# The mixing product of three quarters of the spectrum in rounded passes instead of exact fp32, with the hand-written order of all engines replaced

## The chip, the cores and the metric

The kernel runs on one core of one Trainium2 chip. The metric is the device time of one execution in microseconds (us). Five engines work side by side in the core: PE (TensorE, matrix products, with PEld for the loading of its stationary operand), DVE (VectorE), ACT (ScalarE), POOL (GpSimd) and SP, which issues DMAs here. They are held together by semaphores.

## The reference

```python
# spectral mixing, x: (8, 1856, 256)
X = np.fft.rfft(x, axis=1)
Yr = Xr @ w_r - Xi @ w_i + b_r
Yi = Xr @ w_i + Xi @ w_r + b_i
Y = soft_shrink(Yr, 0.01) + 1j * soft_shrink(Yi, 0.01)
y = np.fft.irfft(Y, n=1856, axis=1)
# mixture of experts over the 14848 tokens of y
# w_group gives one of 4 groups, w_expert one of its 4 experts
g_idx = np.argmax(x @ w_group, axis=1)
e_idx = np.argmax(xg @ w_expert[g], axis=1)
out[tok] = g_w * e_w * (np.maximum(x[tok] @ w1[g, e], 0) @ w2[g, e])   # F = 1024
```

All of it is float32. The kernel forms the complex product `Xr, Xi` by `w_r, w_i` with three real products: one common product of the difference of two spectra with `wc`, and two products of their own, of which one starts from the common one.

## The kernel before

**Work and stages.** The 8 batches are worked in 4 pairs. The transform of length 1856 is done as 58 by 32, in steps, each named by one letter. For a pair: `c` (`a_mm`, L339) and `d` (`a_turn`, L343) are the first small transform on PE and its transposition by DVE. Then come 8 units, each of two spectral positions (the last of one, so 15 positions a pair). For a unit, `e` (`f_mm`, L618) makes the spectrum on PE in a PSUM tile `bank`; `f` (`f_high`, ACT, L635) copies it rounded to fp32r (a rounded form that PE takes in one pass) into `xh`; `h` (`f_low`, DVE, L640) makes the rest `xl` = spectrum minus `xh`; `i` (`d_copy`, ACT, L645) and `g` (`d_sub`, DVE, L650) make `xd`, the fp32 difference for the common product. For a position, `j` (`m_bias`, ACT, L655) puts the bias into a PSUM tile `pw`; `y` (`m_common`, L661) adds the common product `xd` by `wc` with 2 fp32 matmuls of 256 columns; `z` (`m_share`, DVE, L666) copies it to the other half of `pw`; `k` (`m_mm`, L676) adds the two own products with 12 fp32r matmuls (high by high, high by low, low by high, for two halves of the 256 channels and two products); `m` (ACT, L682) and `o` (DVE, L687) do the shrinkage. With 15 positions in each of 4 pairs there are 60 common products.

After that a pair is transformed back: `r` (`b_mm`, L701), `s` (`b_turn`, DVE, L709), `v`, `w`, `x`. `G`, `H`, `R` route the tokens and `S` scatters their numbers into a list for each expert: 128 scatters on POOL, each an indirect DMA of 128 small rows (L248). The first 64 are tied to PE's steps (a scatter waits for the second last step of PE that was written ahead of it, and no more than 3 are on their way), the other 64 are not tied to PE and no more than 5 are on their way. `W`, `V`, `F`, `T`, `X`, `Y`, `U`, `A`, `B`, `D`, `E`, `J`, `K` are weights and 8 early jobs of the experts, begun while the spectrum is still being mixed. The rest of the experts' work follows in loops.

**What sets the order.** Up to about 536 us of the profile, each engine's order is that of a string `ORDER`, one letter a step; the loop over it calls the next step of that letter, and every instruction of the step goes to the end of its engine's queue. Nothing is reordered later, so an instruction that waits holds up all that is behind it on its engine.

```python
for c in ORDER.replace("\n", ""):
    next(steps[c])
```

The common product, whole:

```python
y = psum["m", pr, k][:, 0:D]
for h in range(2):
    nc.tensor.matmul(y, lhsT=units["xd", pr, k // 2][:, h, k % 2, 0], rhs=wc[:, h], start=False, stop=False, ...)
```

`pw`, `xd`, `xh` and `xl` each have two buffers.

Of the kernel before, what the change touches and what calls it, by code (L numbers as in the profile page):

```python
# [9 lines left out]
F32 = mybir.dt.float32  # L10
F32R = mybir.dt.float32r
# [3 lines left out]
ALU = mybir.AluOpType  # L15
# [3 lines left out]
NB, S, D = 8, 1856, 256  # L19
NA, NR = 58, 32  # L20
K1, KP = 30, 32
NP = NB // 2
# [15 lines left out]


ORDER = """  # L40
cddcdcdjcdcldcddcddQdjdcddddeQQfecffhhigiQgcQQyQydQzhkizfkdmmddehgiojfgccoyjyhddzkfdizmhdikgmgeoofccjddyjyhzdkizgkfmmhod
ijefgojcyyhzfkidzkmdgheiojgmocyfjyfhzihkgzikegdmmdoojfeyhjzfhiykigmzokgmjoeyjyzkzflfhikhmgoijefgfhmyzihioggkjemyojyfzhfk
zhiigkgmfmohrojssjfyizyhrkgigmssrzssokemfjfohjihrsyysgigcdcdczddvwxdklvdzwxclxvdkmodwjxxywvzwcxxwwxwddmcGddvoHRRRcRjefly
wxRRdRRhzwkkxefdimhimvRgRgRoRfcojxRwjddxRRRyywzRvwxwRzxvkkRRRwmxxwhRRiRRRmioRgjgRfGoeRRjHhyfRyfzRhzkRkhigRigeSemSSRRmRoo
jffRjyhRSzyRRRRkiShzRSRRRRmSkRReiSfggSojRhiygzSSSmiSRRoRkjgRRyfhmfoSRrzfjhhkiiRsygSgzrmRsskmrSsojeoSsRjyfshfzySrizkkhssi
ggmomvexjovwSwSjwyfxxwySfxzvhvxkwwxzkxSwxhmicwddigGSvomgjoHRxRwlScxRwvwdSjvRxyxSwRRyxedRSzzwcwSffxRhhvRiikwSmdSdRggRxkmS
wRxoRoeffRRRcRRRGdjdhjRRyihgRzSRRRyikzmRRRRHSSllkmReogRoSRfchRjfRidjRhcRySzdiSSygzRRgkkcRdSRmdRomoejRcydSRjdSRyffSzhkRSm
lldizhRdkoRgieSgjyRRRRRmozfRjhRfihSkRieSmggfRSoyjSfRhRhryiRzSiggSSskrzskmojSSssSmroyRssjzyrWezssWkSffhSWmivhixwvSkwgSwgx
vxeomwxSjovwxyVjxfzyhSzwfwSxSkihwkmgVixgmSeffohWjhiSoWgjViGvgvwHyxxyRRzwRxRzRkvwvRRxmRoxRIwRjwexRVyWRwzRRxwxkmoZRfFkRFRh
wGRRRigigRmjWoRRfjHRyhzyRRkmzRRRRRefoRhjRfkhyeSiSmgRzoSRkijRgyRfRmSSRRzokjRhSSSVfiRRShRRmgWySzRoiSSgSSVRRRkjmyRRzRVSRRRR  # L50
koTmSoXRYrUsRRsrASsSSBUSlSsrssVSrASWWUsSsvBSAxlWwSSvxvwxSwwSxwUxvxSwTxwxDBSwVVGWVVSAXIYWHvBxWwWwxRlRRvUxURvwVRRZFAxBwvDw
RAxEwRDWwRFVVxUBFxRURARRDAwVBRJBERRWDWWRRRxDTREXYRRDDRJJRUVEAKRVKRKlRURABBWTURFARWJSUWGVVVRSBXSSAYUBATUHDKRSRRRSDTRBlRWW
RSASRRREBRRUUAJRRKSBXSYSRRDRARDURABRVSUBRDAESUFFJRRBUVDRRRWWDEDVDRXAAWlRJYSREBVWBVTSSUJUWSKKASAVBSSSDBUAUADVSXBDDEBVYUSU
AEASDDSSSBBWUUSSVJSWAWBTSDJXDEAYJBSUEUVJVLADBKEJUAABDUKBDABDDDRKKEEKJKDMJEJKKK
"""

_OFF = {}
# [68 lines left out]
def spectral_moe(ctx: ExitStack, tc: tile.TileContext, x, wri, bri, wgate, w1, w2, cst, out):  # L126
    nc = tc.nc
# [23 lines left out]
    for n in (16,):  # L151
        t = keep.tile([128, NE, n], BF16, name=f"smask{n}")
# [143 lines left out]
    rt = inv.enter_context(tc.tile_pool(name="rt", bufs=1))  # L296
# [4 lines left out]
    cf = fwd.enter_context(tc.tile_pool(name="cf", bufs=1))  # L301
# [4 lines left out]
    T = cf.tile([128, K1, 64], F32, name="T")  # L306
    wf = fwd.enter_context(tc.tile_pool(name="wf", bufs=2))
    pw = fwd.enter_context(tc.tile_pool(name="pw", bufs=2, space=PSUM))

    def banks():  # L310
        return pa.tile([128, 2, 512], F32, name="bank")
# [41 lines left out]
    for _ in range(2):  # L353
        y = pw.tile([128, 512], F32, name="pw")
# [7 lines left out]
    wc = cf.tile([128, 2, D], F32, name="wc")  # L362
# [9 lines left out]
    def weight_steps():  # L372
        nc.scalar.copy(out=sl, in_=craw)
        yield
        nc.vector.tensor_tensor(out=wsum, in0=wraw, in1=wc, op=ALU.add)
        yield
        nc.vector.tensor_tensor(out=wraw, in0=wraw, in1=wc, op=ALU.subtract)
        yield
        for i, w_ in enumerate((wraw, wsum)):
            nc.scalar.copy(out=wh[:, i], in_=w_)  # L380
            yield
            nc.vector.tensor_tensor(out=wl[:, i], in0=w_, in1=wh[:, i].bitcast(F32), op=ALU.subtract)
            yield
        nc.vector.tensor_tensor(out=bias[:, D:], in0=bias[:, D:], in1=bias[:, 0:D], op=ALU.subtract)
        yield
# [10 lines left out]
    wg = ci.tile([128, 8, 64], F32, name="wg")  # L396
    nc.sync.dma_start(out=wg.rearrange("p c m -> p (c m)"), in_=wgate)
    late.close()
    zero = cf.tile([128, 128, 2], F32, name="zero")
    nc.gpsimd.memset(zero, 0.0)  # L400
    with tc.issue_after(x1.ins):
        nc.sync.dma_start(out=lst[0:NE * CAP].rearrange("(p j c) k -> p j (c k)", p=128, j=16),
                          in_=zero[:, 0:CAP // 128].rearrange("p c k -> p (c k)").unsqueeze(1).broadcast_to([128, 16, CAP // 64]))
# [151 lines left out]
    wts, raws, low, units, vs, psum = {}, {}, {}, {}, {}, {}  # L555
# [5 lines left out]
    def steps_of(*dims):  # L561

        def wrap(fn):
            def run():
                for idx in np.ndindex(*[len(d) for d in dims]):
                    fn(*[d[i] for d, i in zip(dims, idx)])
                    yield
            return run()
        return wrap
# [9 lines left out]
    pairs, later, u16, u8, two, k15 = range(NP), range(1, NP), range(16), range(8), range(2), range(15)  # L579

    def load_steps():
        for pr in later[1:]:
            for dc in range(4):
                x_in[pr, dc] = t = xp.tile([128, 32, 64], F32, name="xt")
                nc.sync.dma_start(out=t, in_=x_v[pr, dc])
                yield
        for e in range(NF + 1):
            for i, src in enumerate((w1, w2)):
                raws[e, i] = t = xp.tile([128, 2048], F32, name="xt")
                ins = nc.sync.dma_start(out=t, in_=src[e * 128:e * 128 + 128])  # L590
# [31 lines left out]
    def side(ins, what, pr, kk, h):  # L622
        apart(ins, (what, pr, kk, h), *((o_, pr, kk, 1 - h) for o_ in ("hs" if what in "fc" else "fc")))

    def quad(pr, kk, h):
        return quads(psum["f", pr, kk], kk)[:, h]
# [21 lines left out]
    def d_sub(pr, kk, h):  # L648
        t = units["xd", pr, kk][:, h, 0:min(2, 15 - 2 * kk), 0]
        side(nc.vector.tensor_tensor(out=t, in0=quad(pr, kk, h)[:, :, 0], in1=t, op=ALU.subtract), "s", pr, kk, h)  # L650

    @steps_of(pairs, k15)
    def m_bias(pr, k):
        psum["m", pr, k] = y = pw.tile([128, 512], F32, name="pw")
        nc.scalar.copy(out=y[:, 0:D], in_=bias[:, 0:D])  # L655

    @steps_of(pairs, k15)
    def m_common(pr, k):
        y = psum["m", pr, k][:, 0:D]
        for h in range(2):  # L660
            nc.tensor.matmul(y, lhsT=units["xd", pr, k // 2][:, h, k % 2, 0], rhs=wc[:, h], start=False, stop=False, skip_group_check=True)  # L661

# [230 lines left out]
        store(units.pop(("y", n, t)), lev[j, e], t, "out")  # L893

    w = STAT // 128
    first = []
    xp2 = ctx.enter_context(tc.tile_pool(name="xp2", bufs=3, side="right"))

    @steps_of(range(1))
    def last_lists(_):  # L900
# [7 lines left out]
    def first_rows(_):  # L908
# [2 lines left out]
        nc.gpsimd.tensor_copy(out=first[0].gi, in_=first[0].ent[:, :, 0])  # L911

    steps = dict(
        Q=weight_steps(), l=load_steps(), c=a_mm, d=a_turn, e=f_mm, f=f_high, h=f_low, i=d_copy, g=d_sub, j=m_bias, y=m_common, z=m_share, k=m_mm,
        m=m_relu, o=m_shrink, r=b_mm, s=b_turn,
        v=p_mm, w=p_out, x=p_turn,
        G=g_mm, H=g_turn, R=route_steps(), S=scatter_steps(), W=w_high, V=w_low, I=list_load, Z=list_convert, F=e_fetch, T=e_turn, X=e_high,
# [2 lines left out]
    by_hand = ExitStack()  # L920
    by_hand.enter_context(tc.manual_schedule(engines=engines))
    with ExitStack() as ph, tc.manual_schedule(engines={mybir.EngineType.Pool}):
        done = 0
        for c in ORDER.replace("\n", ""):
            next(steps[c])
            done += c == "o"
            if c == "o" and done == NP * 15:
                fwd.close()
                early["hp"] = ph.enter_context(tc.tile_pool(name="hp", bufs=2))
                early["mp"] = ph.enter_context(tc.tile_pool(name="mp", bufs=1))  # L930
                yp.append(ph.enter_context(tc.tile_pool(name="yp", bufs=6)))
                early["pp"] = ph.enter_context(tc.tile_pool(name="pp", bufs=2, space=PSUM))
        assert not pend and all(next(g, None) is None for c, g in steps.items() if c != "S")
        wts = {e: views(w) for e, w in wts.items()}
# [281 lines left out]
    for i, (kind, q) in enumerate(jobs):  # L1216
# [5 lines left out]
        if i + 2 < len(jobs) and jobs[i + 2][0] == "h":  # L1222
            k = jobs[i + 2][1] + KF - KH
            jw[i + 2], jids[i + 2] = half_load(slice(k, k + 1))
        if i + 1 < len(jobs) and jobs[i + 1][0] == "r":
            k, part = jobs[i + 1][1]
# [49 lines left out]
    with tc.For_i(KF, nfx, 1) as iv:  # L1276
# [9 lines left out]
        hts, h = [], hq.tile([128, 8, 256], F32, name="hh")  # L1286
# [43 lines left out]
```

## Time and profile before

| | before |
|---|---|
| median of 3 runs | 1176.19 us (1174.16 to 1179.11) |
| profiled execution, its own time | 1176.28 us |
| its span in the trace | 1174.5 us |
| mean granted clock of PE | 0.963 |
| PE busy | 1080.0 us, 92% of the span |
| DVE, ACT, POOL busy | 668.8, 482.0, 400.2 us |

The profiled execution stands 0.09 us above the median, and its span leaves 1.8 us of its time outside. PE is the engine to look at: where it stands idle or works slowly, the end may move. A busy share is an average over stages, so the stages are read apart below.

### The profile page before, as it was taken

What the parts mean: (1) busy time and instruction counts of PE and PEld (TensorE: products, weight loads), DVE (VectorE), ACT (ScalarE), POOL (GpSimd) and SP (SyncE); (2) the same over time, 40 slices, a digit from 0 to 9 for tenths busy, and PEclk for the clock granted to TensorE, in tenths of its full rate; (3) what the DMA queues carried; (4) which work ended last, traced back from release to release, by engine and by line L of the source; (5) the groups of instructions that cost most, each with busy time, mean ns of one, the idle gap of its engine ahead of it and who ended that gap; (6) DMA issues with size and microseconds to landing.
All of it is one profiled execution on the core that took longest, in us unless ns stands there. A gap on an engine that the chain in (4) does not pass through costs nothing. (4 is left out here: it accounts for less than half of the span.)

```text
span 1174.5 us, 23221 instructions
## 1 busy us (share of the span) xinstructions
PE 1080.0 (92%) x8944; PEld 896.6 (76%) x8944; DVE 668.8 (57%) x1572; ACT 482.0 (41%) x1222; POOL 400.2 (34%) x497
## 2 busy tenths in 40 slices
PE   7999979988966599879999999999999999999996
PEld 4786755755754378768989999887888888888995
DVE  6779846866765375435655454544554345544532
ACT  2453523532632253223455354444544345443532
POOL 0000132343343526545325333443425333343311
PEclk9999979998998699989999999999999999999999
DMA  9504301620230252104315131553324433313100
GB/s 386 156 3 177 113 1 38 174 72 10 96 105 1 84 205 63 61 28 137 120 56 178 43 112 46 193 193 103 121 85 139 185 113 116 110 52 110 48 23 25
DMA packets 39793, 119.83 MB, mean 102 GB/s; under 512 B 16998, under 2 KB 19305, under 8 KB 31618
## 3 DMA queue, kind: packets, MB, share of 16 engines
q1 hardware_dynamic: 19042, 70.32, 17.4%
q0 software_dynamic: 15744, 31.08, 8.6%
q10 hardware_dynamic: 4896, 16.93, 3.7%
q8 instruction: 71, 1.16, 0.4%
q14 instruction: 40, 0.33, 0.1%
HBM read 84.23 MB, written 34.61 MB: 101 GB/s over the span
## 5 line engine op out<-in xcount | busy, mean ns | idle before, releaser
L540 PE MATMUL py<-big,hh 128*128 128x512 f32 (+1 forms) x848 | 301.0, 396 | 0.0
L478 PE MATMUL ph<-xth,big 128*128 128x384 f32 (+3 forms) x992 | 272.2, 350 | 2.8 <-DVE hl L484 1.2
L541 PE MATMUL py<-big,hl 128*128 128x256 f32 (+1 forms) x848 | 237.1, 280 | 0.0
L248 POOL DMA_INDIRECT lst<-ent,sloti x128 | 126.9, 991 | 294.9 <-PE pw L676 166.0
L484 DVE SCALAR_TENSOR_TENSOR hl<-ph,hh 128x256 fp32r<-128x256 f32 x496 | 159.8, 366 | 81.9 <-ACT hh L482 72.1
L478 PEld LDWEIGHTS ph<-xth,big 128*128 128x128 f32 x992 | 181.1, 188 | 17.1 <-PE ph L478 2.5
L540 PEld LDWEIGHTS py<-big,hh 128*128 128x128 f32 (+1 forms) x848 | 155.8, 184 | 38.1 <-issue 1.6
L482 ACT ACTIVATE hh<-ph 128x256 fp32r<-128x256 f32 x496 | 143.7, 351 | 95.3 <-PE ph L478 88.3
L478 PE MATMUL ph<-xtl,big 128*128 128x384 f32 (+3 forms) x496 | 173.2, 349 | 0.3 <-DVE xtl L466 0.3
L541 PEld LDWEIGHTS py<-big,hl 128*128 128x128 f32 (+1 forms) x848 | 156.1, 184 | 0.2
L525 POOL DMA_INDIRECT out_dram<-yo,si_r x92 | 93.2, 1013 | 174.8 <-DVE yo L548 147.6
L548 DVE SCALAR_TENSOR_TENSOR yo<-py,ent_r,yo 128x256 f32<-128x256 f32 (+1 forms) x92 | 44.4, 483 | 180.6 <-ACT yo L547 166.6
L443 POOL DMA_INDIRECT xg<-ys_d,gi_r x92 | 89.7, 975 | 163.0 <-PE pg L461 129.4
L547 ACT ACTIVATE yo<-py,ent_r 128x256 f32<-128x256 f32 (+1 forms) x92 | 43.7, 475 | 204.1 <-PE py L541 149.5
L478 PEld LDWEIGHTS ph<-xtl,big 128*128 128x128 f32 x496 | 93.4, 188 | 5.3 <-DVE xtl L466 0.6
L676 PE MATMUL pw<-wh,xh 128*128 128x256 f32 x240 | 70.4, 314 | 17.8 <-issue 12.0
L425 DVE TENSOR_TENSOR big<-xt,big 128x512 fp32r<-128x512 f32 x120 | 82.0, 684 | 0.0
L424 ACT CAST big<-xt 128x512 fp32r<-128x512 f32 x120 | 77.0, 641 | 0.0
L618 PE MATMUL bank<-T,big 64*64 64x64 f32 x1920 | 52.1, 229 | 22.3 <-issue 20.2
L618 PEld LDWEIGHTS bank<-T,big 64*64 64x64 f32 x1920 | 42.1, 139 | 36.4 <-issue 28.3
L676 PEld LDWEIGHTS pw<-wh,xh 128*128 128x128 f32 x240 | 47.4, 198 | 29.3 <-issue 14.9
L682 ACT ACTIVATE big<-pw,nlam 128x512 f32<-128x512 f32 x60 | 41.4, 690 | 62.2 <-PE pw L676 55.7
(224 smaller groups left out, 1686.8 us busy)
## 6 DMA issues: line engine op xcount, KB each, us to landing
xt<-in_w_dram SPq DMA_DIRECT2D x38, 1024.0 KB
ys_d<-ysb ACTq DMA_DIRECT2D x32, 512.0 KB
big<-in_x_dram SPq DMA_DIRECT2D x8, 1024.0 KB
xt<-in_x_dram SPq DMA_DIRECT2D x8, 1024.0 KB
big<-in_w_dram SPq DMA_DIRECT2D x8, 1024.0 KB
lst<-ent,sloti POOLq DMA_INDIRECT x128
lst<-zero SPq DMA_DIRECT2D x1, 1920.0 KB
xg<-ys_d,gi_r POOLq DMA_INDIRECT x92
```

What stands on the lines that cost most here:

```text
L248: ins = nc.gpsimd.indirect_dma_start(out=lst, out_offset=bass.IndirectOffsetOnAxis(ap=sl_, axis=0), in_=en_, in_offset=None, bounds_check= ...
L424: nc.scalar.copy(out=wt[:, 2 * i, cs], in_=raws[i][:, cs])
L425: nc.vector.tensor_tensor(out=wt[:, 2 * i + 1, cs], in0=raws[i][:, cs], in1=wt[:, 2 * i, cs].bitcast(F32), op=ALU.subtract)
L443: ins = nc.gpsimd.indirect_dma_start(out=xg[0:m, c, :], out_offset=None, in_=ys_d[0:rows, :], in_offset=bass.IndirectOffsetOnAxis(ap=ids.g ...
L478: nc.tensor.matmul(o[:, :n], lhsT=a_[:, ch, fs], rhs=b_[:, ch, 0:n], start=k == 0, stop=k == 5)
L482: nc.scalar.activation(out=hh[:, f, :m], in_=ov, func=AF.Relu)
L484: nc.vector.scalar_tensor_tensor(out=hl[:, f, :m], in0=ov, scalar=0.0, in1=hh[:, f, :m].bitcast(F32), op0=ALU.max, op1=ALU.subtract)
L525: ins = nc.gpsimd.indirect_dma_start(out=out, out_offset=bass.IndirectOffsetOnAxis(ap=ids.si[0:ids.rows(t), t:t + 1], axis=0), in_=ysb, in ...
L540: nc.tensor.matmul(o, lhsT=hh[:, f, ts], rhs=w2b[:, :, f, :], start=f == 0, stop=f == 7, skip_group_check=True)
L541: nc.tensor.matmul(o[:, 0:D], lhsT=hl[:, f, ts], rhs=w2h[:, f, :], start=False, stop=f == 7, skip_group_check=True)
L618: nc.tensor.matmul(unit[64 * dh:64 * dh + 64, h, c0:c0 + 256].rearrange("p (j c) -> p j c", j=2)[:, :, m:m + 32], lhsT=zys[pr][64 * h:64 * ...
L676: ins = nc.tensor.matmul(y, lhsT=a_[:, h, k % 2, j], rhs=t[:, j, h], start=False, stop=a_ is xl and h == 1, skip_group_check=True)
```

## The change

1. For the first three pairs, except their very first unit, the common product is no longer made with fp32 matmuls. These are 23 units with 43 positions (two positions short of 45). Two new steps a unit make its operand in two parts: `p` (`c_high`, ACT) copies `xd` rounded to fp32r into `xdh`; `q` (`c_low`, POOL) makes the rest `xdl` = `xd` minus `xdh`. `wc` gets the same two parts, once: `wch` on ACT and `wcl` on POOL. `m_common` then does 6 fp32r matmuls (`xdh` by `wch`, `xdh` by `wcl`, `xdl` by `wch`, for two halves) instead of 2 fp32 ones. Pair 3 and the first unit keep fp32.
2. The new tiles lie in a pool `wx`, 12 KB of each partition. It is closed after the 45th common product, and the pool `xp2` (weights of the early jobs) is opened only then.
3. `zero` lies in a tile that routing uses later, and the scratch of the dynamic DMAs is 8192 instead of 16384 bytes.
4. `ORDER` is another string, from its first letter on to about three quarters of it; its last part is much the same. It has 1686 letters instead of 1638: 2 more `Q`, 23 `p`, 23 `q`. The 45th `y` stands at letter 909 (857 before), the first scatter at 479 (469), the 64th at 1074 (1011), the first `F` at 1153 (1074).

```diff
 ORDER = """
-cddcdcdjcdcldcddcddQdjdcddddeQQfecffhhigiQgcQQyQydQzhkizfkdmmddehgiojfgccoyjyhddzkfdizmhdikgmgeoofccjddyjyhzdkizgkfmmhod
+cQcdQdcdcdddcdjddQcdddcddcdjdeeQeffQQhhiiggcyyQQfQhQfizhzkkgidgdcmpmoqjodfcjhyyzikdfzkhiggmpmddoeqofhccjfyjhyiizzggkdmko
...
+    third = ExitStack()
+    wx = third.enter_context(tc.tile_pool(name="wx", bufs=1, side="right"))
+    wch = wx.tile([128, 2, D], F32R, name="wch")
+    wcl = wx.tile([128, 2, D], F32R, name="wcl")
...
     def weight_steps():
         nc.scalar.copy(out=sl, in_=craw)
         yield
+        nc.scalar.copy(out=wch, in_=wc)
+        yield
+        nc.gpsimd.tensor_tensor(out=wcl, in0=wc, in1=wch.bitcast(F32), op=ALU.subtract)
+        yield
...
-    zero = cf.tile([128, 128, 2], F32, name="zero")
+    zero = rt.tile([128, 16, 32], F32, name="L").rearrange("p a b -> p (a b)")[:, 0:256].rearrange("p (c k) -> p c k", k=2)
...
+    split = [(pr, kk) for pr in pairs[:-1] for kk in u8][1:]
+
+    @steps_of(split)
+    def c_high(u):
+        pr, kk = u
+        n = min(2, 15 - 2 * kk)
+        units["xdh", pr, kk] = t = wx.tile([128, 2, 2, 128], F32R, name="xdh", bufs=2)
+        nc.scalar.copy(out=t[:, :, 0:n], in_=units["xd", pr, kk][:, :, 0:n, 0])
+
+    @steps_of(split)
+    def c_low(u):
+        pr, kk = u
+        n = min(2, 15 - 2 * kk)
+        units["xdl", pr, kk] = t = wx.tile([128, 2, 2, 128], F32R, name="xdl", bufs=2)
+        nc.gpsimd.tensor_tensor(out=t[:, :, 0:n], in0=units["xd", pr, kk][:, :, 0:n, 0], in1=units["xdh", pr, kk][:, :, 0:n].bitcast(F32),
+                                op=ALU.subtract)
...
     def m_common(pr, k):
         y = psum["m", pr, k][:, 0:D]
+        if (pr, k // 2) in split:
+            ch, cl = units["xdh", pr, k // 2], units["xdl", pr, k // 2]
+            for a_, ws in ((ch, (wch, wcl)), (cl, (wch,))):
+                for h in range(2):
+                    for t in ws:
+                        nc.tensor.matmul(y, lhsT=a_[:, h, k % 2], rhs=t[:, h], start=False, stop=False, skip_group_check=True)
+            return
...
-    first = []
-    xp2 = ctx.enter_context(tc.tile_pool(name="xp2", bufs=3, side="right"))
+    first, xp2 = [], None
...
+            mixed += c == "y"
+            if c == "y" and mixed == (NP - 1) * 15:
+                third.close()
+                xp2 = ctx.enter_context(tc.tile_pool(name="xp2", bufs=3, side="right"))
...
-    nc = _bacc.Bacc("TRN2", target_bir_lowering=False, num_devices=1)
+    nc = _bacc.Bacc("TRN2", target_bir_lowering=False, num_devices=1, dynamic_dma_scratch_size=8192)
```

On PE, this is the second unit of pair 0 in the program of before: its spectrum, a piece of the next pair's first transform, and the first of its two positions' products (`xd` is the operand of the common product, `xh` and `xl` those of the own products).

```order
L618 MATMUL bank<-T,big 64x2x32 x32
L339 MATMUL bank<-big,cA 64x512 x8
L661 MATMUL pw<-wc,xd 128x256 x4
L676 MATMUL pw<-wh,xh 128x256
L676 MATMUL pw<-wl,xh 128x256
L676 MATMUL pw<-wh,xh 128x256
L676 MATMUL pw<-wl,xh 128x256
L676 MATMUL pw<-wh,xl 128x256 x2
```

And this is the same unit in the changed program, from the same piece of the first transform on.

```order
L344 MATMUL bank<-big,cA 64x512 x8
L691 MATMUL pw<-wch,xdh 128x256
L691 MATMUL pw<-wcl,xdh 128x256
L691 MATMUL pw<-wch,xdh 128x256
L691 MATMUL pw<-wcl,xdh 128x256
L691 MATMUL pw<-wch,xdl 128x256 x2
L691 MATMUL pw<-wch,xdh 128x256
L691 MATMUL pw<-wcl,xdh 128x256
L691 MATMUL pw<-wch,xdl 128x256 x2
L709 MATMUL pw<-wh,xh 128x256
```

The four fp32 matmuls of a unit's two positions (L661) have become twelve fp32r matmuls (L691), at the same place in the unit.

On POOL, this is what stood between the start of the program and the first 31 scatters before (`ent` and `sloti` are the entries of the lists and their places; a row ending in x7 stands for seven like it).

```order
L400 MEMSET zero 128x256
L205 ISA
L205 TENSOR_SCALAR ent<-K 128x16
L248 DMA lst<-ent,sloti 245888x2 x7
L205 TENSOR_SCALAR ent<-K 128x16
L248 DMA lst<-ent,sloti 245888x2 x24
```

In the changed program this stands there, up to the sixth scatter.

```order
L409 MEMSET L 128x256
L382 ISA
L382 TENSOR_TENSOR wcl<-wc,wch 128x512
L675 TENSOR_TENSOR xdl<-xd,xdh 128x512 x6
L675 TENSOR_TENSOR xdl<-xd,xdh 128x2x128
L675 TENSOR_TENSOR xdl<-xd,xdh 128x512 x5
L206 TENSOR_SCALAR ent<-K 128x16
L675 TENSOR_TENSOR xdl<-xd,xdh 128x512
L249 DMA lst<-ent,sloti 245888x2 x3
L675 TENSOR_TENSOR xdl<-xd,xdh 128x512
L249 DMA lst<-ent,sloti 245888x2 x3
```

Thirteen of the 23 subtractions stand ahead of all scatters; the other ten stand between scatters, in the whole program behind 3, 6, 8, 12, 18, 25, 30, 32, 37 and 40 of them. After the last of them come 24 scatters in a row.

On ACT, this is the first place of `c_high` in the changed program, and what stands around it (L715 is the shrinkage of the unit before, L681 the bias).

```order
L654 COPY xd<-bank 128x256 x2
L715 ACTIVATE big<-pw,nlam 128x512
L668 CAST xdh<-xd 128x512
L715 ACTIVATE big<-pw,nlam 128x512
L681 COPY pw<-bias 128x256
L644 CAST xh<-bank 128x512
```

The rounding of a unit's difference stands here behind a shrinkage that waits for PE's products of the unit before.

## Rows read from the trace of the kernel before

**Rows 1.** The page's head and its first part: busy time of each engine.
```profile
span 1174.5 us, 23221 instructions
PE 1080.0 (92%) x8944; PEld 896.6 (76%) x8944; DVE 668.8 (57%) x1572; ACT 482.0 (41%) x1222; POOL 400.2 (34%) x497
```

**Rows 2.** Busy time by stage: PE, PEld, DVE, ACT, POOL, then PEclk, DMA share, GB/s.
```profile
0.00:140.00 140.00, 131.56 (x1947) 94.53 (x1948) 112.43 (x220) 61.97 (x133) 0.77 (x6) 1.00 0.48 175
140.00:312.00 172.00, 148.74 (x1862) 104.63 (x1860) 112.49 (x238) 63.40 (x137) 63.77 (x67) 0.90 0.22 63
312.00:400.00 88.00, 56.46 (x680) 41.71 (x678) 48.01 (x111) 24.38 (x55) 37.45 (x43) 0.83 0.14 44
400.00:536.00 136.00, 119.12 (x910) 101.06 (x910) 72.46 (x150) 49.44 (x98) 64.81 (x77) 0.93 0.31 100
536.00:1174.00 638.00, 624.15 (x3553) 554.66 (x3552) 323.44 (x857) 282.82 (x802) 233.37 (x305) 1.00 0.31 105
```

**Rows 3.** PE's waits after 536 us, the longest first.
```profile
PE pg L1078 <- DVE tab L1079: 1.3, 1, 1.3
```

**Rows 4.** PE's waits in 0 to 536 us: us in total, times, longest.
```profile
PE bank L701 <- DVE big L709: 13.1, 1, 13.1
PE pw L676 <- issue: 12.0, 1, 12.0
...
PE pw L676 <- DVE pw L666: 5.6, 5, 2.6
```

**Rows 5.** Timeline of two places at which PE stops while scatters run.
```profile
346.41 0.98 POOL L248 DMA_INDIRECT lst<-ent,sloti  x1 [0.30 <-issue]
347.69 0.98 POOL L248 DMA_INDIRECT lst<-ent,sloti  x1 [0.30 <-issue]
...
356.34 0.43 DVE L666 TENSOR_TENSOR pw<-pw,bias 128x256 f32<-128x256 f32 x1 [11.48 <-remote]
356.83 0.58 PE L676 MATMUL pw<-wh,xh 128*128 128x256 f32 x1 [12.03 <-issue]
...
395.75 3.21 PE L701 MATMUL bank<-big,CI 32*64 32x512 f32 x22 [13.12 <-DVE big L709]
```

**Rows 6.** The common product's records: duration min/median/max in ns, first and last start.
```profile
L661 PE MATMUL pw<-wc,xd x240: 376/379/793, 24.7 to 366.9; 128*128 128x256 f32 x120
```

**Rows 7.** Timeline of PE in two places: start, duration, instruction (x8 is a run).
```profile
41.82 1.99 PE L661 MATMUL pw<-wc,xd 128*128 128x256 f32 x8
43.48 0.46 PE L676 MATMUL pw<-wh,xh 128*128 128x256 f32 x1
43.77 0.28 PE L676 MATMUL pw<-wl,xh 128*128 128x256 f32 x1
...
44.48 0.28 PE L676 MATMUL pw<-wl,xh 128*128 128x256 f32 x1
...
343.77 1.02 PE L661 MATMUL pw<-wc,xd 128*128 128x256 f32 x4
```

**Rows 8.** The common product alone: busy time and records on PE and PEld by stage.
```profile
0.00:140.00 140.00, 27.22 (x108) 19.14 (x108) 1.00 0.48 175
140.00:312.00 172.00, 28.54 (x96) 18.93 (x96) 0.90 0.22 63
```

**Rows 9.** Groups by line and form: busy us, mean ns, idle before and its releasers.
```profile
L424 ACT CAST big<-xt 128x512 fp32r<-128x512 f32 x120 | 77.0, 641 | 0.0
L425 DVE TENSOR_TENSOR big<-xt,big 128x512 fp32r<-128x512 f32 x120 | 82.0, 684 | 0.0
L248 POOL DMA_INDIRECT lst<-ent,sloti x128 | 126.9, 991 | 294.9 <-PE pw L676 166.0 <-issue 54.0 <-PE bank L720 19.4
L400 POOL MEMSET zero<- 128x256 f32 x1 | 0.3, 312 | 0.3 <-POOLq L1318 0.3
```

**Rows 10.** Timeline at 66 us: a unit's difference, and its common product.
```profile
66.45 0.41 DVE L650 TENSOR_TENSOR xd<-bank,xd 128x256 f32<-128x256 f32 x1
...
67.56 0.48 PE L661 MATMUL pw<-wc,xd 128*128 128x256 f32 x1
```

More of the change, by code (lines that the diff above doesn't have):

```diff
@@ L40 @@
 ORDER = """
-cddcdcdjcdcldcddcddQdjdcddddeQQfecffhhigiQgcQQyQydQzhkizfkdmmddehgiojfgccoyjyhddzkfdizmhdikgmgeoofccjddyjyhzdkizgkfmmhod
-ijefgojcyyhzfkidzkmdgheiojgmocyfjyfhzihkgzikegdmmdoojfeyhjzfhiykigmzokgmjoeyjyzkzflfhikhmgoijefgfhmyzihioggkjemyojyfzhfk
-zhiigkgmfmohrojssjfyizyhrkgigmssrzssokemfjfohjihrsyysgigcdcdczddvwxdklvdzwxclxvdkmodwjxxywvzwcxxwwxwddmcGddvoHRRRcRjefly
-wxRRdRRhzwkkxefdimhimvRgRgRoRfcojxRwjddxRRRyywzRvwxwRzxvkkRRRwmxxwhRRiRRRmioRgjgRfGoeRRjHhyfRyfzRhzkRkhigRigeSemSSRRmRoo
@@ L45 @@
[L45 to L54, printed above, removed]
+cQcdQdcdcdddcdjddQcdddcddcdjdeeQeffQQhhiiggcyyQQfQhQfizhzkkgidgdcmpmoqjodfcjhyyzikdfzkhiggmpmddoeqofhccjfyjhyiizzggkdmko
@@ new lines @@
+dpdemojqffcyjhzyzkhiidmgkegpomeddojcqfhflhijyzydizkggkpdmocmjofhqjeylfyzihgizgkkddpmqmoejfohfyjyhiizzggpkmkfohjeqyfihimz
+ggopkmojjqyyfzzhfkikhgigrmopmjosseqjyfyfhihzirggsspkzmrkqeossmrjoffyhjhisgiycgsclpdcqzzdddkdvdcxmwxwovlxddjvwwkxxwwymxzc
+vdedxwwcxoddffhGihgcigHRddRvpRjRvxcRwRwyRdxzkkxwwRmmdeRxvRooRxRfvqhjwjRyRRyzwRiRxRlwikmzRRRxxwkRRgmoRRgpGRRejqfRojyHRRyS
+hzffhhzSSkiimggpRkRRqReoRRmjRoRSeSfjRyyzSfRkhiRzRRhigRRRkgRempfRqohjRySmiiRRRgSzRgRoRpqfRjkSSmhofyfhihSijzggSRrsskmypzrq
+SSRosSskmrSRojjSesSlffshhyyzrizgkskismgopmvwRqxxvSwSoevxjwjxxwwyySSwvzxffkzxkwxhmSwimhcogdGSiSgjdovvHRxpwRwcxljqwxRddRef
@@ new lines @@
+ySSxRyRhRzfShwivRizwckRxRgxwmRkgdRmdvwSRxwexSRRfoocdpjfjGqRRhyRidRRRhiRRgzRygSRzpSkqRHRkcmRRRReSSomojSSffRjScddhydzRRyih
+RkRzRiggmkdpmRqoSSjllcSeRfcoRddyjfRyhzhzRilkRgdimRRgdpoqkRRRRjRSmSRefyoRRzSjfhikRhRiggRmeffoyRjhhrziigSRgRSysSSkzrksmssr
+oemsjSsfShfoijyrWSWyhzSisSsSSgSgkvzmWvkoxRWjVwwxwvSmxxwvweyVoSxSxSjzffywhWwkzSVSSimhxxkoewgffmihhoiigjGggHSRjRRvvySywxRR
+wRRwzkxRmRxvxwoRRzvRjxwxxWRRReykzRwRRwkxVfmmhiojiVgRIgoGywjWWVRRRHzRyfZRkFRRzFRhRRSeSSmofRRjRhSkfSSyRhmzeSoRkRiSigjSfgSm
+RSyRRhfzioRRhjRliRSgkgymzRoRjRRRSkRRSRymRRzRkmoRRRRoTXSYRVSRrssVSUArSSsSrBsSsUrsRUAWBSAsSsWWvSvSvSSBSSWSwxxxlwwSwvxxwSxw
@@ L55 @@
+wUxTwxVVWVAXVBDYWGvHvxlRwwVUUxDxAVwWRIBRURRxZEJAVBRwRvvwxRFRWRRxRVUwARDKRWARRDBBDDRWFERJwTDDVFxRRXwYFVRUEARRxlWWRUABERRT
+BUUFARRAXBRSYWBRSGSWVUAHJDVVBURRUVRRlWRSSASRJVDBEUTARKRJBRWRDRSRADDXYBSWUVRRRSRSRVRWURRWKSKSDASERRDBRJFRlWTVSABSRUARURRD
+BXERAYKBWWKDUUSJASSATBBUUSSDXABDAEVVDWSSYEEWJJSBUSDAUSVTSBAUBJASUADVDKDVSXEEYSSBUVSBDJUAAJBUDSBAUKADDBKKEDBDEELKKDJJDJEM
+KJKKRK
 """
@@ L913, in spectral_moe @@
     steps = dict(
-        Q=weight_steps(), l=load_steps(), c=a_mm, d=a_turn, e=f_mm, f=f_high, h=f_low, i=d_copy, g=d_sub, j=m_bias, y=m_common, z=m_share, k=m_mm,
+        Q=weight_steps(), l=load_steps(), c=a_mm, d=a_turn, e=f_mm, f=f_high, h=f_low, i=d_copy, g=d_sub, j=m_bias, p=c_high, q=c_low, y=m_common, z=m_share, k=m_mm,
         m=m_relu, o=m_shrink, r=b_mm, s=b_turn,
@@ L922, in spectral_moe @@
     with ExitStack() as ph, tc.manual_schedule(engines={mybir.EngineType.Pool}):
-        done = 0
+        done = mixed = 0
         for c in ORDER.replace("\n", ""):
```

## The prediction

> **What bounds the kernel now.** I read the busy times first, then the busy times by stage, then PE's waits, and last the timeline at the places that these point to. PE is busy for 1080.0 of 1174.5 us [rows 1]. By stage, PE stands idle for 8.4 us before 140 us, 23.3 us in 140 to 312, 31.5 us in 312 to 400, 16.9 us in 400 to 536, and 13.8 us in the 638 us after that (length less busy time) [rows 2]. So the first 140 us and the last 638 us are PE's: what is taken from PE's work there comes off the end. Between them some 72 us of PE time are lost to waits. The chain of work that ended last does not help, since it breaks off at the last store; the stages do.
>
> The change acts before 312 us, and its gain has to pass through the stages behind. Two things say that it will. In 536 to 1174 us PE's longest kind of wait is 1.3 us in total [rows 3], so the experts' part is a block of PE work that begins earlier if what stands before it ends earlier. And in 140 to 536 us everything follows one written order, in which the scatters are tied to PE's steps: if PE is early, they are.
>
> The two longest stops are of another kind: 12.0 us and 13.1 us, once each [rows 4], both while scatters run one after the other on POOL [rows 5]. In them DVE's wait carries no engine's name ("remote", 11.48 us), and DVE and PE start again within half a microsecond of each other. I take them as signals of PE that arrive late while POOL sends scatters; the profile does not show why.
>
> **The common product on PE.** A position has four records of it (240 for 60) [rows 6]. A run of eight, two positions, takes 1.99 us in one place; with the last record's own 0.38 us taken off, that is (1.99 - 0.38) / 7 = 0.230 us from one to the next, or 0.92 us a position. A run of four in another place gives (1.02 - 0.38) / 3 = 0.213 us, or 0.85 us [rows 6, 7]. What replaces it has the form of the own products, which stand right behind: six steps from 43.77 to 44.48 us, 0.118 us each [rows 7], so six cost 0.71 us. A position saves 0.14 to 0.21 us; 43 of them save 6.2 to 9.1 us, and in the middle 7.6 us.
>
> The Trainium skill ("FP8 and Floating Point Precision", TensorE Precision Notes) says that true fp32 takes four passes through the array. By it the three passes left would save a quarter of the product, an estimate of 0.25 x 0.85 x 43 = 9.2 us; the rows have 0.71 of 0.85 to 0.92, 17% to 23%. I keep the rows' middle.
>
> Some of these positions run at the lower of PE's two clock levels (1.2 and 2.4 GHz). Before 140 us the granted clock is 1.00, and 108 records, 27 positions, lie there; in 140 to 312 us it is 0.90 [rows 2, 8], a fifth of the time at the half level. Of the 43 changed positions some 18 lie in that stage: 18 x 0.2 x 0.175 = 0.6 us more (0 to 1.2). Together PE saves 8.2 us.
>
> **The work on ACT and POOL.** `c_high` is a copy of 128x512 with rounding. The same operation takes 0.64 us elsewhere [rows 9]; 23 of them are 14.7 us of ACT's time, in stages in which it is busy 62 of 140 and 63 of 172 us [rows 2]. This costs nothing in itself, as ACT's idle time covers it. Without that cover it would be 14.7 us. `c_low` on POOL has no row of its kind in that size. Below, DVE does the same operation in 0.68 us [rows 9]. Above I take the time from one scatter to the next, 347.69 - 346.41 = 1.28 us [rows 5]. POOL's own filling of 128x256 takes 0.31 us [rows 9], 0.62 us for twice the elements; with two inputs to read in place of none I put it at twice that, 1.2 us. 23 of them are 28 us on an engine that is busy for 0.8 us of the first 140 and 64 of the next 172 [rows 2]: time in plenty. `wch` and `wcl` come once, before any common product that needs them: nothing, since PE has the first unit's fp32 products to do meanwhile (at worst 0.64 + 1.2 us).
>
> The Trainium skill ("GPSIMD Engine Reference", Performance versus the Vector engine) gives some 2.6 cycles an element for an operation with two inputs, an estimate of 1.1 us here. No run so far shows it.
>
> **The longer chain.** So far `xd` is complete at 66.45 + 0.41 = 66.86 us, and its first product stands at 67.56 us, 0.70 us later [rows 10]. Now ACT's 0.64 us and POOL's 1.2 us lie between them, 1.9 us with nothing for the handing over. ACT keeps its written order, so `c_high` can stand behind a shrinkage that waits for PE; if it is late, `c_low` is, and PE stops ahead of the products with everything behind them. POOL, too: ten of the 23 subtractions stand behind scatters that wait for PE's steps, and a scatter holds POOL for 1.28 us. What such a wait costs is not in the trace. Its lower bound is nothing, where the order leaves room. The upper is 0.3 us a unit, a little under a sixth of the 1.9 us, 23 x 0.3 = 7 us. The nearest row is the wait of a position's own products for DVE's step between the two products, the same kind of short chain out of PE's results: 5.6 us for 60 positions [rows 4], 0.093 us each. By that 23 units wait 2.1 us. I take this value.
>
> **The rest.** `wx` gives its room to `xp2` after the 45th common product. The transfers into `xp2` stand later in both orders, and the DMA share is 0.22 and 0.14 of the time there [rows 2], so I cost it at nothing; if one came late, it would delay an early job by some microseconds, in a stage in which PE has the back transform to do. The smaller scratch touches POOL's DMAs alone: nothing, if 8192 bytes hold what is on its way. The new order as such I take as neutral, with both signs in the rivals.
>
> **Sum.** 1176.28 - 8.2 + 2.1 = **1170.2 us**, 0.5% under before. 0.5%, 5.9 us, is about what a measurement of this kernel tells from no change, with runs between 1174.16 and 1179.11 us.
>
> **The rivals.**
> - *The gain goes into waits.* The chain through ACT and POOL costs its upper bound, 7 us, or PE's saved time turns into idle time in 140 to 400 us, where PE already waits 55 us. For it: in 140 to 312 us ACT and POOL have neighbours that wait for PE. Against it: 25 of the 43 positions lie before 140 us, where POOL is empty. 1176.28 - 8.2 + 7 = 1175; 1175 to 1178.
> - *One more stop.* The only mechanism here that ends slower: a train of scatters delays PE's signals so far that a third stop like the 13.1 us comes about. In the new order the subtractions stand among the scatters, and 24 scatters stand in a row after the last one; if the subtractions hold scatters back until they run bunched, PE stops where it ran on. It decides from 12 us on: 1170.2 + 13.1 = 1183.
> - *One stop fewer.* The same mechanism the other way: the new order has work ready for PE ahead of a train, or the scatters at another place. 1170.2 - 12.5 = 1158.
> - *The scratch is too small.* Each scatter would have to wait for the room of earlier ones. If the step of 1.28 us became 2, the 64 scatters not tied to PE would cost 64 x 0.72 = 46 us on POOL, of which half might be hidden: 1190 or more. Against it: no more than 5 are on their way.
> - *The change does less than it says:* the six small matmuls run slower than 0.118 us, as each needs a weight load of its own. They stand next to twelve of exactly that kind at 0.118 us, so I give it no chance apart; it would end at 1175 as well.
>
> **How the numbers follow.** The forecast has 0.50, gain into waits 0.20, one stop more 0.12, one stop fewer 0.13, the scratch 0.05. The forecast's own range is its terms' bounds: 1176.28 - 9.1 - 1.2 = 1166 to 1176.28 - 6.2 + 7 = 1177. For eight in ten I need the forecast, the waits and part of both cases of a stop: 1160 to 1183. Leaving out the scratch, most of the fewer stop and half of the further one leaves out no more than 0.2. Faster by over 0.5% means under 1170.3: a little over half of the forecast and all of the fewer stop, 0.28 + 0.13, about 0.41. Slower by over 0.5% means over 1182.1: the scratch, most of the further stop, a rest of the waits, 0.17. The same: 0.42.
>
> **What would show it.** The run of six at L691 should step by 0.118 us, so twelve take about 1.4 us a unit. `c_low` should take 0.7 to 1.3 us. PE's idle time before 140 us should stay within 3 us of 8.4 us, and the last 638 us should keep their length and begin 6 us earlier. The prediction is wrong if PE waits for POOL's `xdl` by more than 7 us in all, if the number of stops over 10 us is not two, or if scatters step by more than 1.28 us.

## The result, and the profile after

The changed kernel takes 1181.22 us (1175.65 to 1185.04), the kernel before 1175.71 us in the same comparison: ratio 1.0051, 95% interval 1.0035 to 1.0066. It is 0.5% slower, where 0.5% faster was forecast. The profiled execution has a span of 1178.5 us, 4.0 us more than before [rows 1]. Two executions far above all others of their kernel, 2100 us in e1 and 3593 us in the new order in fp32 of e8, are left out of the ratios below.

The changed kernel's page: its head, and the busy times.

```profile
span 1178.5 us, 23472 instructions
PE 1078.1 (91%) x9030; PEld 899.9 (76%) x9030; DVE 670.3 (57%) x1572; ACT 494.7 (42%) x1246; POOL 430.9 (37%) x521
```

Its busy time by stage, in the columns of [rows 2]; the block of the experts begins 4 us later, so the last two stages are cut at 540 us.

```profile
0.00:140.00 140.00, 131.10 (x2080) 98.06 (x2083) 116.15 (x228) 72.43 (x152) 22.48 (x24) 1.00 0.51 175
140.00:312.00 172.00, 143.82 (x1757) 101.37 (x1748) 106.89 (x223) 63.39 (x138) 66.55 (x70) 0.87 0.19 57
312.00:400.00 88.00, 62.98 (x760) 47.60 (x758) 52.02 (x121) 26.50 (x59) 38.08 (x44) 0.83 0.22 67
400.00:540.00 140.00, 113.33 (x877) 95.28 (x878) 71.30 (x145) 48.40 (x95) 68.28 (x75) 0.89 0.28 88
540.00:1178.00 638.00, 626.82 (x3574) 557.63 (x3573) 323.89 (x859) 283.96 (x804) 235.54 (x311) 1.00 0.31 106
```

In the first 140 us PE does 133 more instructions in nearly the same busy time (50 of them are the six small matmuls in place of four records), and idles 8.9 us instead of 8.4. What is lost is lost between 140 and 540 us: 28.2 us idle in 140 to 312 (23.3 before), 26.7 in 400 to 540 (16.9 in a stage 4 us shorter), and the granted clock is 0.87 and 0.89 there instead of 0.90 and 0.93 [rows 2]. In 312 to 400 us PE idles less than before, 25.0 us instead of 31.5. The last 638 us hold PE work as before, 3574 instructions (3553).

PE's waits up to 540 us, for [rows 4].

```profile
PE pw L709 <- DVE pw L699: 26.4, 8, 17.1
PE bank L627 <- issue: 14.0, 29, 1.8
PE ph L877 <- issue: 8.8, 4, 7.0
PE ph L877 <- DVE hl L889: 8.0, 1, 8.0
PE pw L691 <- ACT pw L681: 6.6, 3, 3.6
```

In place of stops of 12.0 and 13.1 us there are stops of 17.1, 8.0 and 7.0 us, and one of 3.6 us for ACT's bias. One stop is over 10 us; any number but two was a sign that the prediction is wrong. No row names a wait for POOL's `xdl`. The longest stop, in the timeline:

```profile
359.18 0.98 POOL L249 DMA_INDIRECT lst<-ent,sloti  x1 [0.30 <-issue]
360.47 0.98 POOL L249 DMA_INDIRECT lst<-ent,sloti  x1 [0.30 <-issue]
...
362.27 0.37 ACT L644 CAST xh<-bank 128x256 fp32r<-128x256 f32 x1 [15.15 <-remote]
...
364.41 0.42 DVE L649 TENSOR_TENSOR xl<-bank,xh 128x256 fp32r<-128x256 f32 x1 [16.01 <-remote]
...
366.98 0.58 PE L709 MATMUL pw<-wh,xh 128*128 128x256 f32 x1 [17.06 <-DVE pw L699]
```

Fourteen scatters run one after the other from 343.60 to 361.5 us, a train, and two more follow. ACT waits 15.15 us for PE's spectrum and goes on at 362.27 us, 0.8 us after the fourteenth; but PE has done nothing since 366.98 - 17.06 = 349.92 us, so what ACT waited for was done by then. It is the picture of [rows 5], with a longer stop. The train begins with the 65th scatter, and the two stops of [rows 5] also lie in trains of the second 64, which are not tied to PE's steps.

The new operations. First a unit's twelve matmuls, then `c_low` and `c_high` (duration min/median/max in ns).

```profile
38.48 0.39 PE L691 MATMUL pw<-wch,xdh 128*128 128x256 f32 x1
38.70 0.28 PE L691 MATMUL pw<-wcl,xdh 128*128 128x256 f32 x1
38.82 0.28 PE L691 MATMUL pw<-wch,xdh 128*128 128x256 f32 x1
...
40.00 0.36 PE L709 MATMUL pw<-wh,xh 128*128 128x256 f32 x1
40.20 0.28 PE L709 MATMUL pw<-wl,xh 128*128 128x256 f32 x1
```

```profile
L675 POOL TENSOR_TENSOR xdl<-xd,xdh x23: 725/1285/1300, 29.2 to 257.1; 128x512 fp32r<-128x512 f32 x20, 128x256 fp32r<-128x256 f32 x3
```

```profile
L668 ACT CAST xdh<-xd x23: 396/619/622, 28.5 to 256.6; 128x512 fp32r<-128x512 f32 x20, 128x256 fp32r<-128x256 f32 x3
```

From the first product of a unit to the second own product it takes 40.20 - 38.48 = 1.72 us; before, 43.77 - 41.82 = 1.95 us [rows 7]. A unit of two positions saves 0.23 us, not 0.35. The step inside is 0.118 us as forecast; but the first step takes 0.22 us and the change to the own products 0.20. The forecast's 0.230 us for an fp32 record had the first step of its block in it, and the forecast left out the longer first step of the new block.

### The profile page after: what moved, and what is told of

Same layout as the page of the kernel before. It is cut to its first block, busy times and chain, and to the rows that moved or that the text cites. A ratio compares the mean times of both kernels' runs of the same rounds, so it can differ in the third digit from the quotient of the medians.

```text
span 1178.5 us, 23472 instructions
## 1 busy us (share of the span) xinstructions
PE 1078.1 (91%) x9030; PEld 899.9 (76%) x9030; DVE 670.3 (57%) x1572; ACT 494.7 (42%) x1246; POOL 430.9 (37%) x521
## 5 line engine op out<-in xcount | busy, mean ns | idle before, releaser
L675 POOL TENSOR_TENSOR xdl<-xd,xdh 128x512 fp32r<-128x512 f32 (+1 forms) x23 | 27.9, 1213 | 137.9 <-ACT xdh L668 102.6
L877 PE MATMUL ph<-xth,big 128*128 128x256 f32 x256 | 52.8, 294 | 16.3 <-issue 8.1
L709 PE MATMUL pw<-wl,xh 128*128 128x256 f32 x240 | 66.4, 296 | 0.0
```

Of the source, the lines that this page charges most:

```text
L709: ins = nc.tensor.matmul(y, lhsT=a_[:, h, k % 2, j], rhs=t[:, j, h], start=False, stop=a_ is xl and h == 1, skip_group_check=True)
L877: ins = nc.tensor.matmul(o[:, i * 256:(i + 1) * 256], lhsT=a_[:, ch, fs], rhs=b_[:, ch, :], start=k == 0, stop=k == 5)
```

## The experiments

**Theory A.** The passes are saved, and the new order loses more than that in how it meets the trains of scatters, during which signals come late. **Theory B.** The split, or the order, costs something by itself: ACT's and POOL's work, late differences, the smaller scratch.

**One change at a time (e1, e2).** e1 has the new order without `p` and `q`; e2 has the order of before, with `p` and `q` behind each unit's second `g`.

```diff
-    split = [(pr, kk) for pr in pairs[:-1] for kk in u8][1:]
+    split = []                              # e1, ORDER without p and q
-...igojfgccoyjyhddzkf...
+...igojfgpqccoyjyhddzkf...                 # e2, ORDER of before
```

> The changed kernel with the new order, but every common product in fp32 again (no rounding step, no subtraction on POOL). Theory A (PE does save its 8 us up to 265 us, and the new order then loses more in stops during the trains of scatters): without the saving it is slower than the changed kernel by about the 5 to 8 us that the passes are worth, 1184 to 1190 us, and the stops of 17, 8 and 7 us stay at the trains. Theory B (the split itself costs: ACT and POOL work, late differences): it is as fast as before or faster, 1170 to 1177 us.

> The changed kernel, but with the order of before, into which the rounding and the subtraction of a unit are put directly behind its second difference step. Theory A: the passes are saved, the order loses nothing of its own except that the common product stands closer to its operand than in the new order: PE waits for POOL's difference, up to 1.9 us a unit; 1168 to 1180 us, and two long stops at the same trains. Theory B: slower than the changed kernel, over 1182 us, because the split is what costs.

e1: 1177.64 us against 1168.6, ratio 1.0070 (1.0050 to 1.0089). e2: 1165.48 us, 0.9976 (0.9956 to 0.9996). The order alone is slower than before, and the split alone is a little faster than before, though PE waits 8.0 us for `xdl` in e2. Multiplied, the two ratios give 1.0046; the whole change has 1.0051. Theory B falls for the split on this chip. e1 lies under its range, as before itself is 7 us faster on this chip; and by these ratios the split is worth 2 to 3 us with late signals, not the 5 to 8 us that I expected. PE's longest waits in e1 show stops like those of the changed kernel, without any split:

```profile
PE bank L626 <- issue: 19.2, 47, 1.8
PE pw L708 <- DVE pw L698: 18.7, 5, 14.4
PE ph L876 <- issue: 7.8, 6, 5.7
PE ph L876 <- DVE hl L888: 6.6, 1, 6.6
```

**Without scatters (e3).** Both kernels, on the same chip as e1 and e2. The lists stay empty here and in e4 and e5, so the experts' DMAs move less, too: 104.5 MB in all instead of 119.8.

```diff
             sl_, en_ = pend.pop(0)
+            continue
```

> The kernel before without its 128 scatters (the lists of the experts stay empty, all else is done). Theory A: the stops of 12 and 13 us and the later ones go, PE's semaphores arrive in time in 140 to 540 us, and PE's granted clock stays high there: 25 to 50 us less than before, 1125 to 1150 us. Theory B (the stops come from the order, and the trains only happen to be there): within 10 us of before.

> The changed kernel without its 128 scatters (the lists stay empty, all else is done). Theory A: the difference of the two kernels turns round, this one is 6 to 9 us faster than the kernel before without scatters, as the passes alone are worth. Theory B (split or order cost by themselves): it is 0 to 8 us slower than the kernel before without scatters.

The kernel before: 1063.08 us, 0.9087 (0.9071 to 0.9104). The changed one: 1057.26 us, 0.9035 (0.9018 to 0.9052). The sign turns: without scatters the change is worth 5.8 us, a little under the 6 to 9 expected. And 128 scatters cost the kernel before 105 us, twice what I had expected at most. Its page without them:

```profile
span 1060.4 us, 22904 instructions
PE 1034.7 (98%) x8944; PEld 867.5 (82%) x8944; DVE 667.1 (63%) x1572; ACT 482.2 (45%) x1222; POOL 275.5 (26%) x369
```

Against the profile of before [rows 1], which is of the first chip, PE's idle time falls from 94.5 to 25.7 us and its busy time by 45.3 us, with the mean granted clock at 0.996 instead of 0.963.

**POOL busy without a DMA, fewer scatters on their way, half the scratch (e4 to e7).** e4 is e1 without scatters. e5 is the changed kernel with a filling in place of each scatter, e6 the changed kernel with another bound, e7 the kernel before with the smaller scratch.

```diff
-            ins = nc.gpsimd.indirect_dma_start(out=lst, ...)
+            ins = nc.gpsimd.memset(fill, 0.0)                                  # e5
-            late_, way = len(sent) >= 64, 5 if len(sent) >= 64 else 3
+            late_, way = len(sent) >= 64, 2                                    # e6
-    nc = _bacc.Bacc("TRN2", ..., num_devices=1)
+    nc = _bacc.Bacc("TRN2", ..., num_devices=1, dynamic_dma_scratch_size=8192) # e7
```

> The new order with fp32 common products (as e1), and without the 128 scatters (the lists stay empty). Theory A (the new order is worse only in how it meets the trains of scatters): as fast as the kernel before without scatters, 1063 us within 3, and the changed kernel without scatters is 5 to 9 us faster than this one, the worth of the passes. Theory B (the new order has a fault of its own): 5 to 10 us slower than the kernel before without scatters.

> The changed kernel with each scatter replaced by a filling of 128x800 on POOL, some 1 us, with the same waits for PE's steps (the lists stay empty). Theory A in the form that the scatter's DMA holds up the other engines' signals: near the changed kernel without scatters, 1055 to 1065 us, and no stop of PE over 3 us. Rival: it is POOL being busy, with the subtractions queued behind waiting scatters, that costs: 1085 us or more.

> The changed kernel with no more than 2 scatters on their way, in place of 3 and later 5. If the length of an unbroken train decides how long a signal is held up, the trains have gaps and the stops of 17, 8 and 7 us shrink: 1160 to 1175 us. If every scatter delays signals by the same, or the lists come too late for the experts' early jobs: 1180 us or more.

> The kernel before with 8192 bytes of scratch for the dynamic DMAs instead of 16384, nothing else. Theory A: no change, within 0.3% of before. Rival (the smaller scratch is what costs): 5 us slower or more, with a step from scatter to scatter of more than 1.28 us.

These ran on another chip, and there the kernel before, with all its scatters, takes 1060.69 us. So the expectations that leaned on 1176 us can't be read; only the ratios to before on that chip can. e7: 0.9980 (0.9970 to 0.9991), so the scratch costs nothing here; e2, which is faster than before with late signals, has the smaller scratch as well. e6: 1.0233 (1.0214 to 1.0251). PE waits 13.6 us for an early job's rows there, 13.1 at once, which is about half of the 25 us: the lists come too late. e4: 1054.64 us, e5: 1049.95 us, both below their ranges. Between e4 and e5 lies the split alone, with POOL busy for 0.77 us in place of each scatter: 4.7 us, where 21.5 units at 0.23 us make 4.9. PE never waits for `xdl` in e5. The new order without scatters is 0.6% faster than before with them; before without them was not run on this chip.

**The two kinds of chip (e8, f1, f2).** The changed kernel (e8, f1, f2), the new order in fp32 (the same), the old order with the split (e8), and a copy of before (f1), on three more chips.

> The changed kernel itself, beside the two single changes on one chip. Two kinds of chip have been met: on one the kernel before takes 1168 to 1176 us and the signals of PE, ACT and DVE come late during scatters, on the other it takes 1061 us and none is late. Theory A: on a chip with late signals it is 0.3 to 0.8% slower than before, as measured first; on a chip with prompt signals it is 0.5 to 1.2% faster, as the passes and the order are then worth what the runs without scatters gave. Theory B (the split or the order costs anyway): not faster on either.

> The new order with fp32 common products, as e1. Theory A: on a chip with late signals 0.5 to 0.9% slower than before; with prompt signals 0.2 to 0.7% faster. The changed kernel is faster than this one by 0.2% with late and by 0.3 to 0.7% with prompt signals. Theory B: slower than before on both.

> The old order with the split, as e2. Theory A: 0.1 to 0.5% faster than before with late signals; with prompt signals 0 to 0.5% faster, less than the passes, since the common product stands close behind its operand. Theory B: not faster than before.

> A copy of the kernel before. Its ratio is 1.000 within 0.2% on any chip; its profile shows whether signals of PE, ACT and DVE come late during the scatters on this chip (time near 1170 us) or in time (near 1060 us).

> The changed kernel. Where signals come late: 1.003 to 1.007 of before. Where they are in time: 0.995 to 1.001. If the trains of scatters are not what decides between the two, there is no such link between the lateness in the profile and the ratio.

> The new order with fp32 common products. Where signals come late: 1.005 to 1.009, so slower than the changed kernel by the 2 us that the split then brings. In time: 0.996 to 0.999.

> The changed kernel. If signals come late here (before near 1170 us): 1.003 to 1.007 of before, with its stops of PE at the trains of scatters. If they are in time (before near 1061 us): 0.996 to 1.000.

> The new order with fp32 common products. If signals come late here: 1.005 to 1.009 of before, some 2 us slower than the changed kernel. If in time: 0.996 to 0.999.

All three had signals in time, as had the chip of e4 to e7. Each chip was met in one comparison only, so it is not shown whether the lateness belongs to a chip or to the time at which it was met. Ratios to before on the same chip:

| | late signals | in time: e8 | f1 | f2 |
|---|---|---|---|---|
| before, median us | 1175.71 (result), 1168.6 (e1, e2) | 1060.32 | 1061.06 | 1060.34 |
| copy of before | | | 0.9995 (0.9985 to 1.0006) | |
| changed | 1.0051 | 0.9988 (0.9974 to 1.0003) | 0.9969 (0.9958 to 0.9981) | 0.9980 (0.9972 to 0.9989) |
| new order, fp32 | 1.0070 | 0.9974 (0.9960 to 0.9988) | 0.9963 (0.9950 to 0.9976) | 0.9974 (0.9962 to 0.9987) |
| old order, split | 0.9976 | 1.0220 (1.0198 to 1.0242) | | |

Two expectations missed. The changed kernel of e8 was to be 0.5 to 1.2% faster with signals in time and is 0.1% faster, not clear of nothing. The old order with the split was to be up to 0.5% faster and is 2.2% slower. So the two single changes, which add up with late signals, don't add up here.

The copy's rows stand against [rows 1, 2, 4] as follows: the page, then the stages, then PE's longest waits up to 430 us.

```profile
span 1061.3 us, 23221 instructions
PE 1032.6 (97%) x8944; PEld 870.3 (82%) x8944; DVE 668.9 (63%) x1572; ACT 486.6 (46%) x1222; POOL 402.7 (38%) x497
```

```profile
140.00:240.00 100.00, 98.58 (x1529) 72.22 (x1528) 93.39 (x209) 50.23 (x112) 49.32 (x52) 1.00 0.30 87
240.00:312.00 72.00, 69.06 (x1024) 51.85 (x1017) 65.70 (x140) 37.39 (x82) 42.26 (x47) 1.00 0.27 84
```

```profile
PE bank L753 <- DVE yt L742: 5.4, 1, 5.4
PE pw L676 <- DVE pw L666: 2.3, 5, 0.5
```

The same instructions in the same order, and PE is 98.6% and 95.9% busy in 140 to 312 us, where it was busy for 148.74 of 172 us, 86%. The scatters themselves are no quicker. First the profile of before, then the copy; in each, POOL's work on them, and its waits for an earlier one to land (us in total, times, longest):

```profile
L248 POOL DMA_INDIRECT lst<-ent,sloti x128: 969/980/1277, 141.8 to 505.7; - x128
POOL lst L248 <- DMA lst<-ent,sloti: 8.6, 7, 3.8
```

```profile
L248 POOL DMA_INDIRECT lst<-ent,sloti x128: 966/979/1495, 141.7 to 412.5; - x128
POOL lst L248 <- DMA lst<-ent,sloti: 25.5, 18, 5.8
```

The medians are 980 and 979 ns. Under the same bounds on those on their way, POOL waits less for landings where signals are late, so a later landing of the scatters is not what those profiles show. Nor is it the train: in the changed kernel on the chip of f2 the 65th scatter and the thirteen behind it follow each other by the same steps of 1.29 to 1.35 us, from 282.79 us on, and no engine waits without a name. What differs is the wait without an engine's name: over its whole span the copy has no such row among its waits, while the profiled execution of before has seven. Four of them:

```profile
ACT hh L852 <- remote: 19.5, 2, 15.7
DVE big L709 <- remote: 19.0, 3, 14.9
DVE pw L666 <- remote: 17.4, 3, 11.5
ACT xh L635 <- remote: 14.4, 3, 8.3
```

**Why the split brings nothing where signals are in time (e9, and the early split of f1).** In the changed kernel on the chip of f2, POOL and then PE:

```profile
215.16 0.97 POOL L249 DMA_INDIRECT lst<-ent,sloti  x1 [4.23 <-DMA lst<-ent,sloti]
216.13 1.29 POOL L675 TENSOR_TENSOR xdl<-xd,xdh 128x512 fp32r<-128x512 f32 x1
...
217.48 0.50 PE L691 MATMUL pw<-wch,xdl 128*128 128x256 f32 x2 [2.21 <-POOL xdl L675]
```

A scatter waits 4.23 us for an earlier one to land, the subtraction stands behind it, and PE stops for 2.21 us in the middle of a unit. Such stops of PE sum to 2.8 us in this execution; in the old order with the split (e8) to 16.2 us, two thirds of its 24 us; its granted clock is lower, too, 0.984 instead of the copy's 0.993. With fillings in place of scatters (e5) there is no such stop, and the split is worth its 4.7 us. So these stops take 2.1 to 2.8 us of what the passes save in the changed kernel; the rest of the loss is not accounted for. Two kernels keep the split only for the units whose subtraction stands ahead of the first scatter: e9 in the old order (14 units), the other in the new one (13 units, 25 positions).

```diff
-    split = [(pr, kk) for pr in pairs[:-1] for kk in u8][1:]
+    split = [(pr, kk) for pr in pairs[:-1] for kk in u8][1:15]   # e9, old order
+    split = [(pr, kk) for pr in pairs[:-1] for kk in u8][1:14]   # f1, new order
```

> The old order, and the split only for the 14 units whose subtraction on POOL stands ahead of the first scatter; the other units keep fp32. If the subtractions among the scatters cost PE more than their passes bring, it is 0.1 to 0.4% faster than the old order with the full split; if not, it is slower than that one by the 16 positions' passes, 2 to 3 us.

> The new order, and the split only for the 13 units whose subtraction stands ahead of the first scatter. If the subtractions queued between scatters take the rest of the gain, it is faster than both the changed kernel and the fp32 form of the same order: 0.992 to 0.996 with signals in time, by the passes of 25 positions, 0.112 us each. With late signals it is 1.003 to 1.007, as the order decides. If they cost nothing, it is slower than the changed kernel by 2 us.

e9: 1.0030 (1.0017 to 1.0044): 1.9% better than the full split in that order, more than the 0.1 to 0.4% expected, and still no gain. In its first 140 us PE is busy for 129.71 us where the copy of before has 133.11. No scatter runs there yet, and PE waits 1.1 us for `xdl` and 0.6 us for `xdh`: half of the 3.4 us come from the new chain, as the old order puts the product close behind it. The early split in the new order: 1056.25 us, 0.9943 (0.9926 to 0.9961). It beats before on a chip with signals in time. That it beats the fp32 form beside it is not shown: that one has 1056.16 us and 0.9963, and the intervals overlap, as do those with the changed kernel. On a chip with late signals it was not run.

## Why the prediction was wrong

- **The step that failed is the new order, which I took as neutral.** With late signals it costs 0.7% (e1), about 8 us, and the split gives back 2 to 3 us (e1 against the result, across chips; e2). The same order is 0.3% faster where signals are in time. So the order has no fault by itself; it loses where signals are held up during the scatters. Which of its many differences makes it lose more there than the old order is not shown.
- **The rival "one more stop" had the right place and the wrong form.** There are not three stops of 12 us, but one of 17.1, two of 7 to 8, and more of 3 to 4. That its price, 1183 us, comes near the measured 1181.22 is luck. The prediction also let the scatters follow PE's steps up to 536 us; that holds for the first 64 only, and the long stops lie among the others. My reading of the two stops in [rows 5], signals of PE that come late, was right, but too narrow: ACT's and DVE's waits are without a name too, and I counted two stops where the scatters cost 105 us in all (e3). I saw 72 us of waits between 140 and 536 us and did not ask how much of it had this one cause.
- **The clock takes a part.** 0.963 of 1174.5 us leaves 43.5 us of full speed unused, 0.954 of 1178.5 us leaves 54.2. The stages in which it fell are those in which PE's idle time grew. Not all of these 10.7 us cost time: PE's busy time falls by 1.9 us in place of the 4.9 us of passes saved, so its work takes some 3.0 us longer, an estimate. Its idle time grows by 5.9 us, from 94.5 to 100.4, and 5.9 - 1.9 is the 4.0 us of the span. The prediction counted a gain at the lower level (0.6 us) and not that PE would spend more time there.
- **The passes were mis-sized.** 0.14 to 0.21 us a position were forecast, 7.6 us in all; a unit's rows give 0.23 us, 4.9 us in all, and e4 against e5 4.7 us. The Trainium skill ("FP8 and Floating Point Precision", TensorE Precision Notes) counts four passes for true fp32, and by that the estimate was 9.2 us. The trace does not bear the estimate out (9.1 us by its own factors), since 0.23 of 1.95 us is 12%, not a quarter: three small matmuls step by 3 x 0.118 = 0.354 us inside a block, an fp32 one by its two records, 2 x 0.213 = 0.426, and each block costs more at its edges.
- **The longer chain** was put at 2.1 us. In the changed kernel's first profile no row has PE wait for `xdl`; with signals in time the wait is 2.1 us (f1) and 2.8 us (f2). That the size agrees is luck: it was 0.093 us at each of 23 units, and the traces have one or two stops of up to 2.2 us. The place, subtractions behind scatters, was named, but without a price.
- **Right:** 0.118 us a step, `c_high` 0.62 us (0.64), `c_low` 1.285 us (1.2), the scratch without a cost (e7), and the last 638 us, which keep their length (but begin 4 us later, not 6 earlier).

Open: why some chips hold up signals during scatters of small rows. All that the runs show is that the scatters are needed for it (e3), that POOL's work on a scatter takes the same time on both kinds, and that trains of the same step stand on both. Many of the late signals come near the end of a train or up to 5 us after it, but not all: in the profile of before ACT goes on in the middle of one, with scatters until 360.6 us:

```profile
351.42 0.37 ACT L635 CAST xh<-bank 128x256 fp32r<-128x256 f32 x1 [8.27 <-remote]
```

Whether it is the scatter's DMA or POOL's work on it is not shown, as a filling in its place was run only where signals are in time. Wider gaps between scatters were not tried on a chip that holds them up. And every execution here was also recorded by the profiler; whether signals are as late without that is not known.

## What to carry to other kernels

When PE waits for a signal that its neighbour should have sent long ago, add up all waits of that kind before costing any other edit: here one cause stood behind 105 us, and it decided the sign of a change that had nothing to do with it. Take the cost of a form of matmul from the first instruction of its block to the second one of the next block, not from the steps inside. A new step on a queue that holds waiting DMAs is as late as the DMA ahead of it, so give that wait a price of its own. And compare two kernels on more than one chip: the ratio here was 1.0051 on one and 0.9969 to 0.9988 on three others.

## What the runs showed of the hardware

- The same kernel took 1168.6 to 1176 us on two chips and 1060 to 1061 us on four others, each met once, with the same durations of POOL's DMA instructions (medians of 980 and 979 ns).
- On the first kind, ACT and DVE have waits without a name of up to 18.8 us (e2) in or just behind trains of scatters; on the second none stands in the profiles, with trains of the same step.
- A block of matmuls costs more at its edges than inside. From the first product of an fp32 block to the second own product it takes 1.95 us, or 1.83 without the own product's step of 0.118 us, where eight inner steps of 0.213 us would make 1.70 [rows 7]. For the block of twelve small matmuls these are 1.72, 1.60 and 12 x 0.118 = 1.42 us, so it pays more at its edges, and the saving shrinks.
